# Key layouts made from one PSUM copy, and x tiles of the second layer pair turned by DMA, in a two-pair spectral and attention kernel

## The chip, the cores and the metric

The kernel runs on one core of a Trainium2 chip. The metric is device time in microseconds (us) of one execution; the kernel before takes 1351.86 us as the median of 4 runs (1351.64 to 1351.93). One of these executions, 1351.93 us, was also profiled, and all traces shown come from it.

## The reference: what is computed

The input x is 2048 rows by 512 columns in bf16. Two pairs of layers follow each other, and each layer adds its result to x. Weights are shared by the two pairs.

```python
x = A_x
x = x + _A_ref(_layernorm(x, axis=-1), A_w_r, A_w_i)
x = x + _B_ref(_layernorm(x, axis=-1), B_wq, B_wk, B_wv, B_wo)
x = x + _A_ref(_layernorm(x, axis=-1), A_w_r, A_w_i)
x = x + _B_ref(_layernorm(x, axis=-1), B_wq, B_wk, B_wv, B_wo)
```

`_A_ref` is a spectral filter: a real two-dimensional FFT over rows and columns, a product with the complex weight w_r + i w_i, and the inverse FFT. `_B_ref` is attention with 32 query heads of width 16 over one shared key and one shared value head, softmax over all 2048 keys, and an output projection:

```python
q = (lambda x, *d: x.transpose(*d))((x @ wq).reshape(B, S, H, Dh), 0, 2, 1, 3)
k = x @ wk
v = x @ wv
scores = jnp.einsum("bhqd,bkd->bhqk", q, k) * (Dh ** -0.5)
p = _softmax(scores, axis=-1)
o = jnp.einsum("bhqk,bkd->bhqd", p, v)
```

## The kernel before, in words

**Data.** x stays in SBUF as `x_sb`, [128 partitions, R = 4, T = 4, 512]: 16 tiles of 128 rows, addressed (t, r). There are eight PSUM banks: two double banks `sa`, and four single banks `b` (NB = 4). The bulk of the SBUF scratch is a pool `w4`; 13 small buffers `e2` hold exponentials and, for short times, other things; a pool `xnt` of six buffers holds normalised tiles.

**The spectral layer (A).** The front works on pairs of tiles. `tr_x` (L1064) turns two tiles with eight TensorE transposes into one `b` bank, `tr_evac` (L1070, which copies through the helper at L1236) takes them to an `e2` buffer, and `mm1` (L1076) multiplies each turned tile with the table PH, four matmuls into one `b` bank. `mm1_evac` (L1084) takes that out on ScalarE with the layer norm's scale, which comes from the statistics `bn` (L1015, VectorE) and `rstd` (L1030, ScalarE). Four tiles of one t are combined on VectorE (`radix_g`). The middle (`mid`, `filt`, `radix_d`) transforms along the rows, filters, and starts the inverse; the back (`inv`, `radix_v`, `y_mm`) finishes it and adds the result to x. For each t the back then normalises (`apply`, L1040, VectorE), turns again (`tr_n`, L1229), and makes keys, queries and values.

**The keys.** `k_mm` (L1249) makes, for the 512 rows of one t, a bank in which the 16 key rows are repeated eight times over the partitions. `k_evac` (L1253) takes that bank out twice, once into KA and once into KB, each time with a 0/1 column `part` that keeps the even or the odd groups of 16 partitions. One of the two is run on ScalarE and one on VectorE, whichever the planner finds free (`flex`, L797; ScalarE's form is L1256, VectorE's L1258). This happens for t = 0 to 3 in each pair of layers. Values follow (`v_mm`, `v_evac` with L1270 and L1272).

**The attention layer (B).** There are 32 blocks (four query stretches qb, four groups g, two parities), and each takes 16 key tiles times four heads, a unit being one 128x512 score tile. ScalarE takes two units at a time from an `sa` bank and exponentiates them (L1297). VectorE takes one unit from a `b` bank and makes a power-of-two approximation of the exponential from integer arithmetic (L1304); GpSimd adds two further phases of it (L1308). TensorE makes scores (L1292) and multiplies with the values (L1314) into one accumulator bank per block. When a block is done its bank is taken out by L1321. When four groups of a qb are done, `close_rows` (L879) projects (L1345), adds to x (L1227, `close_x`), and in the first pair starts the next layer's front on those rows, while attention goes on. So the front of the second pair runs inside the first attention for t = 0, 1, 2, and after it for t = 3.

**What sets the order.** Nothing is scheduled by hand: `Plan` simulates the engines with fixed durations, and emits each instruction when its simulated engine would start it. Every engine then executes its own list in order. Tasks are added with `add`: an engine or several (`ways`), a duration, dependencies, `take` (a PSUM bank it needs) and `give` (a bank it releases), `prio` and `order`. `both` (L188) releases a bank once two tasks have ended. `bg_next` (L240) picks the next background task; tasks of order above 20 are put back by TIER x (order - 20) / 10 nanoseconds, and the back's orders are 20 + 10 t and up. `pe_next` (L380) decides between scores, value matmuls and background matmuls: a background task that would overrun the due time of the next scores is cut into parts that fit, with a tolerance SLIP (100 ns) or, until VectorE has begun on softmax units, SLIP_RAMP (1200 ns). VectorE begins with them (`dve_on`) once the values of all four t are out; I call the time from the first back task to then the ramp. A task that has been late for PATIENT (1000 ns) may go in single parts. `fill` (L454) puts in dummy matmuls (L1002, L1006) to hold the TensorE clock up; one needs a free `b` bank or the accumulator.

**DMA.** SP's queue loads x, the weights, and the tables FT and w (`load_u`, L1103) and IT (`load_it`, L1161) of each pair, and in the last pair writes the output rows from `close_x` (L1351). A DRAM pool `way` of two buffers is declared and not used.

Of the kernel before, what the change touches and what calls it, by code (L numbers as in the profile page):

```python
# [8 lines left out]
ACT = mybir.ActivationFunctionType  # L9
ALU = mybir.AluOpType  # L10
P = 128
BF = mybir.dt.bfloat16
# [3 lines left out]
S, D, H, DH = 2048, 512, 32, 16  # L16
NF = D // 2 + 1
NT = 16
NC = 4
R = 4  # L20
T = 4
# [77 lines left out]
class Task:  # L99
# [5 lines left out]
    def __init__(self, eng, dur, deps, fn, take=None, give=(), then=None, prio=-1, order=0, lazy=0.0, gap=0.0, parts=1, port=False, lock=False, cols=None):  # L105
        self.ways = {eng: dur} if isinstance(eng, str) else dict(zip(eng, dur))
        self.eng, self.deps, self.fn = next(iter(self.ways)), deps, fn
        self.dur = self.ways[self.eng]
        self.take, self.give, self.then = take, give, then
        self.port, self.lock = port, lock  # L110
        self.cols = self.dur * 512.0 / 220.0 if cols is None else cols
        self.prio, self.order, self.lazy, self.gap, self.parts, self.step = prio, order, lazy, gap, parts, 0
        self.end = self.slot = None


class Plan:
# [21 lines left out]
    RAMP_FORCE = 3900.0  # L138
    HOLD = 200.0
    NB = 4  # L140
    TIER = 200.0
    LATE = 0.0
    GAP = 0.0
    SLIP = 100.0
    SLIP_RAMP = 1200.0
    PATIENT = 1000.0
    URGE = 150.0
    TURN = 7000.0
# [91 lines left out]
    def bg_next(self, eng):  # L240
        best = None
        for k in self.bg[eng]:
# [20 lines left out]
            elif eng == "PE" and self.t[eng] - max(ready, k.born) > self.STARVED:  # L263
                prio = -3
            c = (start + self.TIER * max(0, k.order - 20) // 10, prio, k.order, k.seq, start, k)
            if best is None or c[:4] < best[:4]:
# [113 lines left out]
    def pe_next(self):  # L380
# [21 lines left out]
        for b in self.bg_next("PE"):  # L402
            k, n = b[3], 99
            late = T - max(b[5], k.born)
            if kinds and c[0][0] <= b[0] + k.dur + self.PE_SW:
                room = max(limit, c[0][0]) + (self.SLIP if self.at.dve_on else self.SLIP_RAMP) - b[0] - self.PE_SW
                fit = int(room / (k.dur / k.parts)) if room > 0 else 0
# [270 lines left out]
class Layer:  # L678
# [15 lines left out]
    def __init__(self, plan, em, first, last):  # L694
        self.plan, self.em, self.first, self.last = plan, em, first, last
        self.next = None
        self.at = Attn(plan, em, self)
        self.rs = {}
        self.Pk, self.G, self.FT, self.W, self.Dz, self.IT, self.UT, self.V, self.sb, self.xn, self.xt = ({} for _ in range(11))
        self.mm1_done = {}  # L700
        self.g_done = {}
        self.stat = {}
        self.gate = []
        self.two, self.direct = ((x[0] if first else x[1]) for x in (self.TWO, self.DIRECT))
        self.sd_of = {}
# [95 lines left out]
    def add_back(self):  # L801
        p, em, at = self.plan, self.em, self.at
        left = [T]
        for t in range(T):
            o = 20 + 10 * t
            cs = []
            for b in range(2):
                es = []
                for j in range(2):
                    if t == 0 and not self.direct:  # L810
                        m = p.add("PE", 440.0, [self.mid[2 * j]], lambda k, t=t, b=b, j=j: em.inv(self, t, b, j, k.slot, (0,)),
                                  take="b", order=o)
                        n = p.add("PE", 440.0, [m, self.mid[2 * j + 1]],
                                  lambda k, t=t, b=b, j=j, m=m: em.inv(self, t, b, j, m.slot, (1,)), order=o)
                    elif t == 0:
                        m = p.add("PE", 880.0, [self.fil[2 * j]], lambda k, b=b, j=j: em.inv0(self, b, j, k.slot, 0),
                                  take="b", order=o)
                        n = p.add("PE", 880.0, [m, self.fil[2 * j + 1]],
                                  lambda k, b=b, j=j, m=m: em.inv0(self, b, j, m.slot, 1), order=o)
                    else:  # L820
                        n = m = p.add("PE", 880.0, self.mid, lambda k, s, t=t, b=b, j=j: em.inv(self, t, b, j, k.slot, (s,)),
                                      parts=2, take="b", order=o)
                    es.append(p.add(*self.flex(t, 482.0, 600.0), [n], lambda k, t=t, b=b, j=j, m=m: em.inv_evac(self, t, b, j, m.slot, k.eng),
                                    give=(m,), order=o))
# [3 lines left out]
            for j in range(0, R, w):  # L828
                key, ks = ("b", t, j), []
                for i, r in enumerate(range(j, j + w)):  # L830
                    put = t in self.FIRST_PUT
                    n = 5 if put else 4
                    y = p.add("PE", 217.0 * n, cs, lambda k, s, t=t, r=r, n=n: em.y_mm(self, t, r, k.slot, s, n), parts=n, take="b",
                              order=o + 1)
                    if put:
                        c = p.add("ACT", 482.0, [y], lambda k, t=t, r=r, y=y: em.put_x(t, r, y.slot), order=o + 1)
# [5 lines left out]
                    z = p.add("DVE", 597.0, [y], lambda k, t=t, r=r, y=y: em.add_x(t, r, y.slot), give=(y,), order=o + 1)  # L842
                    ks.append(p.add("DVE", 795.0, [z], lambda k, key=key, i=i, t=t, r=r, w=w: em.bn(self, key, i, (t, r), w),
                                    order=o + 2))
# [4 lines left out]
                for a in range(j, j + w, 2):  # L849
# [3 lines left out]
                                    lambda k, t=t, a=a, x=x: em.trn_evac(self, t, a, x.slot, k.eng), give=(x,), order=o + 4))  # L853

            def k_got(k, t, i):
                at.k_ready[(t, i)] = k.end + p.LAT[k.eng]
# [7 lines left out]

            m = p.add("PE", 870.0, te, lambda k, s, t=t: em.k_mm(self, t, k.slot, s), parts=4, take="b", order=o + 5)
            last = []
            for i in range(2):
                last.append(p.add(*self.flex(t, 586.0, 667.0), [m], lambda k, t=t, i=i, m=m: em.k_evac(t, i, m.slot, k.eng), order=o + 5))
            p.both(*last, m, lambda k, t=t, last=last: k_got(k, t, last.index(k)))
            if t == 0:  # L870
                at.add_qt((0, 0), te, o + 5)
            m = p.add("PE", 800.0, te, lambda k, s, t=t: em.v_mm(self, t, k.slot, s), parts=4, cols=256.0, take="b", order=o + 6)
# [6 lines left out]
    def close_rows(self, qb, deps):  # L879
        p, em, at = self.plan, self.em, self.at  # L880
        t = qb
        if not self.last and t == T - 1:
            p.ranked(1)
        rows = []
        for r in range(R):
            if t == T - 1:
                m = p.add("PE", 660.0, deps[:3] + [self.at.evac_last], lambda k, r=r: em.proj(at, t, r, k.slot, 0, 3), take="b",
                          prio=-2)
                if not self.last and self.PUTC:
                    n = p.add("PE", 434.0, [m, deps[3]], lambda k, r=r, m=m: (em.proj(at, t, r, m.slot, 3, 5), em.mm_x(t, r, m.slot)),  # L890
                              prio=-2)
                    n.put = m
                    rows.append(n)
                    continue
                n = p.add("PE", 220.0, [m, deps[3]], lambda k, r=r, m=m: em.proj(at, t, r, m.slot, 3, 4), prio=-2)
                rows.append(p.add("DVE", 597.0, [n], lambda k, r=r, m=m: em.close_x(self, t, r, m.slot), give=(m,), prio=-2))
                continue
            m = p.add("PE", 870.0, deps, lambda k, s, r=r: em.proj(at, t, r, k.slot, s, s + 1), parts=4, take="b", prio=-2, gap=p.GAP)
            z = p.add("DVE", 597.0, [m], lambda k, r=r, m=m: em.close_x(self, t, r, m.slot), give=(m,), prio=-2)
            rows.append(z)  # L900
        if self.last:
            return
        n = self.next
        w = 2 if t == T - 1 else R
        for j in range(0, R, w):
            n.add_stats(("f", t, j), [(t, r) for r in range(j, j + w)], rows[j:j + w])
        rows = [r.x if hasattr(r, "put") else r for r in rows]
        for j in range(0, R, 2):
            n.add_front([(t, j), (t, j + 1)], rows[j:j + 2], 1)
        if t == T - 1:  # L910
            n.gate = [at.taken]
            n.add_middle()
            n.add_back()
            p.ranks = None


class Emit:
# [130 lines left out]
    def load_x(self, L):  # L1048
        for t in range(T):
            self.nc.sync.dma_start(out=self.x[:, :, t], in_=self.xv[:, :, t])  # L1050

    def load_w(self, L):
        for u in range(2):
            self.load_u(L, u)
        for dst, src in self.w_dma:
            self.nc.sync.dma_start(out=dst, in_=src)
# [193 lines left out]
        self.nc.tensor.matmul(self.ps(slot), lhsT=self.wk8[:, c, :], rhs=self.xTc(L.at, t, c), start=(c == 0), stop=(c == NC - 1),  # L1250
                              skip_group_check=True)

    def k_evac(self, t, i, slot, eng):  # L1253
        out, part = (self.KA, self.KB)[i][:, 512 * t:512 * t + 512], self.part[:, i:i + 1]
        if eng == "ACT":
            self.nc.scalar.activation(out=out, in_=self.ps(slot), func=ACT.Identity, scale=part)  # L1256
        else:
            self.nc.vector.tensor_scalar(out=out, in0=self.ps(slot), scalar1=part, scalar2=None, op0=ALU.mult)  # L1258

    def v_mm(self, L, t, slot, r):  # L1260
        for c in range(NC):
# [174 lines left out]
```

## Time and profile before

| | |
|---|---|
| median of 4 runs | 1351.86 us |
| profiled execution | 1351.93 us |
| its span, first to last instruction | 1350.1 us |
| granted TensorE clock | 1.000 |
| PE busy | 1311.2 us (97%) |
| DVE busy | 1299.9 us (96%) |
| ACT busy | 1224.9 us (91%) |
| POOL busy | 850.6 us (63%) |
| DMA moved | 22.02 MB, mean 16 GB/s |

PE is TensorE, DVE VectorE, ACT ScalarE, POOL GpSimd, SP SyncE; PEld is TensorE's weight load, which overlaps PE. Matmuls are pipelined and PE's busy time includes dummies, so 97% does not say that TensorE is at its peak. A line such as L1236 can be a helper that several tasks use; the tile names left of the arrow tell which. The stages can be told from the busy digits: the first pair's spectral work until about 58 us, its ramp to 110, its attention to 686; the second pair's spectral work to 730, ramp to 782, attention to 1340, and a short end. Lines of a timeline give the start in us, the length in us, engine, line, operation, output and input, count, and in brackets the idle time just before and what ended it. A length is that of a group of merged instructions where the count is over one.

### The profile page before, as it was taken

The numbers are of one execution on the slowest core, as the hardware profiler recorded it, in microseconds if no ns is written. First come the engines' busy times: TensorE is split into PE (matmuls) and PEld (weight loads), VectorE is DVE, ScalarE is ACT, GpSimd is POOL, SyncE is SP. The second block draws the span as 40 slices with busy tenths as digits, with TensorE's granted clock in tenths as the row PEclk, the third lists the DMA queues.
The fourth block names the chain that finished last, engine by engine and source line by source line (L and its number), as shares of the span: only waits on it lengthen the run. The fifth ranks groups of instructions, "written<-read, shape, count | busy, mean of one in ns | idle before, by whom it ended". The sixth has DMA issues, their size and how long they took to land.

```text
span 1350.1 us, 31719 instructions
## 1 busy us (share of the span) xinstructions
PE 1311.2 (97%) x13051; PEld 429.5 (32%) x13118; DVE 1299.9 (96%) x2328; ACT 1224.9 (91%) x1390; POOL 850.6 (63%) x834
## 2 busy tenths in 40 slices
PE   9999999999999999999999999999999999999998
PEld 4642222222223222222246422222222222322222
DVE  6998999999999999999979989999999999999998
ACT  6479999989999899999964799998999999998996
POOL 0005777667776677766820057776777767876775
PEclk9999999999999999999999999999999999999999
DMA  9100000000000000000051000000000000000000
GB/s 290 40 1 1 2 1 2 2 1 1 2 1 2 1 2 2 1 1 2 2 164 40 1 1 2 2 2 17 1 2 1 6 13 2 1 1 18 1 2 17
DMA packets 21073, 22.02 MB, mean 16 GB/s; under 512 B 2240, under 2 KB 19648, under 8 KB 20928
## 3 DMA queue, kind: packets, MB, share of 16 engines
q1 hardware_dynamic: 20640, 19.44, 4.6%
q8 instruction: 102, 1.67, 0.5%
q10 hardware_dynamic: 288, 0.56, 0.1%
q14 instruction: 43, 0.35, 0.1%
HBM read 17.89 MB, written 2.10 MB: 15 GB/s over the span
## 4 chain that ended last, share of the span: by engine, by line
DVE 33%; ACT 31%; PE 30%; issue 3%; DMA 1%; SPq 1%; POOL 0%; POOLq 0%; DVEq 0%
ACT e L1297 31%; DVE w L1304 22%; PE b L1314 12%; PE sa L1292 6%; PE b L1292 6%; DVE st L1020 2%; DVE w L1149 1%; DVE x_sb L1227 1%; PE b L1345 1%; PE b L1276 1%; DVE raw L1321 1%; PE b L1078 1%; PE b L1176 1%; DVE on L1332 1%; DVE xd L58 1%
## 5 line engine op out<-in xcount | busy, mean ns | idle before, releaser
L1297 ACT ACTIVATE e<-sa 128x1024 bf16<-128x1024 f32 x1228 | 1138.5, 1080 | 34.3 <-PE sa L1292 27.1
L1308 POOL INT64_ADD w<-w x818 | 847.6, 1048 | 480.4 <-DVE w L1304 436.0
L1304 DVE TENSOR_SCALAR w<-b 128x512 uint16<-128x512 f32 x1640 | 1000.9, 679 | 8.1 <-PE b L1292 2.9
L1314 PE MATMUL b<-w,vs 128*32 128x512 bf16 x4920 | 543.3, 385 | 4.2 <-DVE w L1310 1.1
L1314 PE MATMUL b<-e,vs 128*32 128x512 bf16 x2456 | 406.1, 386 | 0.3
L1292 PE MATMUL b<-w,KB 32*128 32x512 bf16 x852 | 262.2, 381 | 3.3 <-DVE w L1304 1.2
L1292 PE MATMUL sa<-w,KA 32*128 32x512 bf16 x1260 | 258.0, 382 | 5.8 <-ACT e L1297 3.4
L1292 PE MATMUL sa<-w,KB 32*128 32x512 bf16 x1196 | 248.0, 381 | 5.4 <-ACT e L1297 2.3
L1314 PEld LDWEIGHTS <-vs 128*32 128x32 bf16 x7376 | 144.3, 94 | 338.4 <-issue 322.5
L1292 PE MATMUL b<-w,KA 32*128 32x512 bf16 x788 | 232.1, 381 | 0.5
L1292 PEld LDWEIGHTS <-KA 32*128 32x128 bf16 x2048 | 81.0, 91 | 226.0 <-issue 217.6
L1292 PEld LDWEIGHTS <-KB 32*128 32x128 bf16 x2048 | 82.4, 91 | 221.7 <-issue 217.0
L1321 DVE STREAM_TRANSPOSE raw<-b 128x512 f32<-128x512 f32 x64 | 45.2, 706 | 2.4 <-PE b L1314 2.4
L1020 DVE BATCH_NORM_STATS2 st<-x_sb 128x6 f32<-128x512 bf16 x52 | 35.4, 681 | 4.8 <-DMA x_sb<-in_A_x_dram 4.3
L1227 DVE TENSOR_TENSOR x_sb<-b,x_sb 128x512 bf16<-128x512 f32 x52 | 34.5, 678 | 3.5 <-PE b L1345 2.7
L1276 PE MATMUL b<-gx,wq 128*128 128x512 bf16 x103 | 34.6, 385 | 0.6
L1345 PE MATMUL b<-WO,w 128*128 128x512 bf16 x114 | 33.2, 382 | 0.8 <-DVE w L1341 0.2
L1176 PE MATMUL b<-it,xd 128*128 128x256 bf16 x256 | 30.8, 273 | 3.2 <-DVE xd L58 3.2
L1216 PE MATMUL b<-tab_PS,w 128*128 128x512 bf16 x120 | 31.5, 379 | 1.2 <-DVE KB L1258 0.8
L1078 PE MATMUL b<-tab_PH,e 128*128 128x512 bf16 x119 | 30.5, 380 | 1.7 <-ACT w L1091 0.3
L1236 ACT CAST e<-b 128x512 bf16<-128x512 f32 x30 | 17.1, 586 | 15.0 <-PE b L1176 9.8
L1091 ACT ACTIVATE w<-b,sb 128x512 bf16<-128x512 f32 x32 | 21.3, 689 | 9.5 <-PE b L1078 8.0
(84 smaller groups left out, 590.1 us busy)
## 6 DMA issues: line engine op xcount, KB each, us to landing
it<-const_IT SPq DMA_DIRECT2D x8, 640.0 KB, 6.3
w<-const_FT SPq DMA_DIRECT2D x8, 512.0 KB, 7.4
x_sb<-in_A_x_dram SPq DMA_DIRECT2D x4, 512.0 KB, 7.5
w<-in_A_w_r_dram SPq DMA_DIRECT2D x8, 256.0 KB, 6.9
w<-in_A_w_i_dram SPq DMA_DIRECT2D x8, 256.0 KB, 7.3
out_dram<-x_sb SPq DMA_DIRECT2D x16, 128.0 KB, 1.8
tab_PH<-const_PH ACTq DMA_DIRECT2D x1, 512.0 KB, 5.7
tab_PS<-const_PS SPq DMA_DIRECT2D x1, 512.0 KB, 7.9
```

The lines of the kernel that those rows point to most:

```text
L1020: self.nc.vector.bn_stats(st, self.ps(slot) if slot else self.x[:, x[1], x[0], :])
L1078: self.nc.tensor.matmul(self.ps(slot), lhsT=xt[:, cc, P * i:P * i + P], rhs=self.PH[:, cc, :], start=(cc == 0), stop=(cc == NC - 1), skip_ ...
L1176: self.nc.tensor.matmul(ps[:, k, :], lhsT=z, rhs=L.IT[t][:, u, w:w + 256], start=(a == 0 and i == 0), stop=(a == 1 and i == 1), skip_group ...
L1227: self.nc.vector.tensor_tensor(out=x, in0=self.ps(slot), in1=x, op=ALU.add)
L1276: self.nc.tensor.matmul(self.ps(slot), lhsT=self.wq[:, c, g * 128:(g + 1) * 128], rhs=self.xTc(at, qb, c), start=(c == 0), stop=(c == NC - ...
L1292: self.nc.tensor.matmul(o, lhsT=KX[rs, kc * P:(kc + 1) * P], rhs=at.QT[qb][rs, g, :], start=True, stop=True, skip_group_check=True)
L1297: self.wrote("ACT", e, self.nc.scalar.activation(out=e, in_=self.ps(slot), func=ACT.Exp, scale=SCALE))
L1304: self.nc.vector.tensor_scalar(out=t[0][:, j], in0=self.ps(slot), scalar1=P1_SCALE, scalar2=P1_BIAS, op0=ALU.mult, op1=ALU.add)
L1308: self.nc.gpsimd.int64_add(t[p][:, 0:n].bitcast(U64), t[0][:, 0:n].bitcast(U64), DELTA[p] * FOUR)
L1314: self.nc.tensor.matmul(self.ps(slot)[32 * h:32 * h + 32, :], lhsT=V[:, kc, :], rhs=rhs, start=first, stop=last, skip_group_check=True)
L1321: self.nc.vector.transpose(out=at.raw[(qb, g)][:, par].rearrange("p a b -> p (a b)"), in_=self.ps(slot))
L1345: self.nc.tensor.matmul(self.ps(slot), lhsT=at.OT[t][:, g, r * P:(r + 1) * P], rhs=self.WO[:, g, :], start=(g == 0), stop=(g == g1 - 1), s ...
```

## The change

Four things change in the text.

1. `k_evac` copies the key bank once, as it is, into a buffer of the `xnt` pool, on ScalarE or VectorE; the bank is released then. Two VectorE instructions (`k_part`) make KA and KB from that SBUF copy. The scores of a t may start when the planner's `k_part` has ended.
2. In the first pair, each pair of rows that `close_rows` closes at t = 0, 1, 2 is written by a DMA from SP to the DRAM pool `way` and read back by a transposing DMA from SP into an `e2` buffer. `add_front` then leaves out `tr_x` and `tr_evac` for that pair; `mm1` is planned from 7 us (TURN, which was there) after the second close. t = 3 is turned by TensorE as before, and so are all tiles of the first pair.
3. TIER goes from 200 to 150.
4. SLIP_RAMP goes from 1200 to 600.

```diff
-    TIER = 200.0
+    TIER = 150.0
...
-    SLIP_RAMP = 1200.0
+    SLIP_RAMP = 600.0
...
             m = p.add("PE", 870.0, te, lambda k, s, t=t: em.k_mm(self, t, k.slot, s), parts=4, take="b", order=o + 5)
             last = []
+            c = p.add(*self.flex(t, 482.0, 600.0), [m], lambda k, t=t, m=m: em.k_evac(self, t, m.slot, k.eng), give=(m,), order=o + 5)
             for i in range(2):
-                last.append(p.add(*self.flex(t, 586.0, 667.0), [m], lambda k, t=t, i=i, m=m: em.k_evac(t, i, m.slot, k.eng), order=o + 5))
-            p.both(*last, m, lambda k, t=t, last=last: k_got(k, t, last.index(k)))
+                p.add("DVE", 323.0, [c], lambda k, t=t, i=i: em.k_part(self, t, i), then=lambda k, t=t, i=i: k_got(k, t, i), order=o + 5)
...
+        turned = [Mark("DMA", None) for _ in range(2)]
+
+        def closed(k):
+            j = rows.index(k) // 2
+            if not self.last and all(z.end is not None for z in rows[2 * j:2 * j + 2]):
+                em.turn_x(self.next, [(t, 2 * j), (t, 2 * j + 1)])
+                turned[j].end = k.end + p.TURN
...
-            z = p.add("DVE", 597.0, [m], lambda k, r=r, m=m: em.close_x(self, t, r, m.slot), give=(m,), prio=-2)
+            z = p.add("DVE", 597.0, [m], lambda k, r=r, m=m: em.close_x(self, t, r, m.slot), give=(m,), then=closed, prio=-2)
...
-            n.add_front([(t, j), (t, j + 1)], rows[j:j + 2], 1)
+            n.add_front([(t, j), (t, j + 1)], rows[j:j + 2], 1, turned[j // 2] if t < T - 1 else None)
...
+    def turned(self, L, tiles, rows):
+        xt = self.t2([NC, 2 * P])
+        self.writer.pop(self.home[id(xt)][0], None)
+        self.nc.sync.dma_start_transpose(out=xt, in_=rows)
+        L.xt[tuple(tiles)] = [xt, 2 * NC]
+
+    def turn_x(self, L, tiles):
+
+        (t, r), _ = tiles
+        way = self.way.tile([2 * P, D], BF, name="way")
+        self.nc.sync.dma_start(out=way.rearrange("(r p) d -> p r d", r=2), in_=self.x[:, r:r + 2, t, :])
+        self.turned(L, tiles, way)
...
-    def k_evac(self, t, i, slot, eng):
-        out, part = (self.KA, self.KB)[i][:, 512 * t:512 * t + 512], self.part[:, i:i + 1]
-        if eng == "ACT":
-            self.nc.scalar.activation(out=out, in_=self.ps(slot), func=ACT.Identity, scale=part)
-        else:
-            self.nc.vector.tensor_scalar(out=out, in0=self.ps(slot), scalar1=part, scalar2=None, op0=ALU.mult)
+    def k_evac(self, L, t, slot, eng):
+        L.K8[t] = self.pool.tile([P, 512], BF, name="xnt", tag="xnt", bufs=6)
+        self.copy(eng, L.K8[t], self.ps(slot))
+
+    def k_part(self, L, t, i):
+
+        self.nc.vector.tensor_scalar(out=(self.KA, self.KB)[i][:, 512 * t:512 * t + 512], in0=L.K8[t], scalar1=self.part[:, i:i + 1],
+                                     scalar2=None, op0=ALU.mult)
```

More of the change, by code (lines that the diff above doesn't have):

```diff
@@ L698, in __init__ @@
         self.rs = {}
-        self.Pk, self.G, self.FT, self.W, self.Dz, self.IT, self.UT, self.V, self.sb, self.xn, self.xt = ({} for _ in range(11))
+        self.Pk, self.G, self.FT, self.W, self.Dz, self.IT, self.UT, self.V, self.sb, self.xn, self.xt, self.K8 = ({} for _ in range(12))
         self.mm1_done = {}
```

## The prediction

> **What bounds the kernel now.** I began with the table by stretch of time, which gives each engine's busy time in windows laid along the stages. Its columns are the window, its length, and then PE, PEld, DVE, ACT and POOL with their instruction counts, the granted clock, the DMA share and GB/s.
>
> ```profile
> 58.00:110.00 52.00, 49.31 (x410) 25.80 (x416) 46.67 (x139) 38.42 (x57) 0.00 (x0) 1.00 0.09 26
> 110.00:262.00 152.00, 149.34 (x1567) 41.86 (x1572) 150.85 (x255) 150.88 (x164) 115.72 (x112) 1.00 0.01 2
> 262.00:304.00 42.00, 40.85 (x392) 12.12 (x396) 41.66 (x75) 34.99 (x41) 25.30 (x27) 1.00 0.01 2
> ...
> 922.00:942.00 20.00, 19.04 (x160) 5.61 (x161) 19.17 (x32) 16.16 (x19) 12.38 (x13) 1.00 0.09 28
> ```
>
> The reader is to see three kinds of stage. In plain attention (110 to 262 us) VectorE and ScalarE are both 99% busy: they share the softmax units, so the two together are the bound and time freed on one is shared out. At a row close of the first attention (262 to 304) VectorE stays full while ScalarE loses 7.0 us. In the ramp (58 to 110) VectorE is nearly full and ScalarE loses 13.6 us, GpSimd does nothing. The granted clock is 1.00 throughout.
>
> Next the page's groups, for what a unit costs, and the rows that the change touches, from the groups kept apart by shape (busy, mean ns, then idle before and its releaser).
>
> ```profile
> L1297 ACT ACTIVATE e<-sa 128x1024 bf16<-128x1024 f32 x1228 | 1138.5, 1080 | 34.3 <-PE sa L1292 27.1
> L1304 DVE TENSOR_SCALAR w<-b 128x512 uint16<-128x512 f32 x1640 | 1000.9, 679 | 8.1 <-PE b L1292 2.9
> ```
> ```profile
> L1236 DVE COPY e<-b 128x1024 bf16<-128x1024 bf16 x8 | 5.4, 680 | 0.5 <-PE b L1068 0.3
> L1256 ACT ACTIVATE KA<-b,part 128x512 bf16<-128x512 f32 x6 | 4.2, 692 | 4.7 <-PE b L1250 4.7
> L1258 DVE TENSOR_SCALAR KB<-b,part 128x512 bf16<-128x512 f32 x6 | 4.5, 748 | 1.0 <-ACT KA L1256 1.0
> ```
>
> Means overlap at their ends, so I take start-to-start intervals from the timeline: 12 exponentials in 11.31 us and 47 in 43.40, that is 0.923 us for two units, 0.462 us a unit on ScalarE; 16 units in 9.81 us on VectorE, 0.609 each. One microsecond freed on VectorE is therefore worth 0.462 / (0.462 + 0.609) = 0.43 us of time, one freed on ScalarE 0.57 us.
>
> Last the timeline at two places: the first row close, and the end of the ramp.
>
> ```profile
> 279.88 0.71 DVE L1321 STREAM_TRANSPOSE raw<-b 128x512 f32<-128x512 f32 x1
> 280.02 0.61 PE L1068 MATMUL b<-tab_ident,x_sb 128*128 128x128 bf16 x8 [0.22 <-DVE w L1304]
> ...
> 281.09 0.67 DVE L1236 COPY e<-b 128x1024 bf16<-128x1024 bf16 x1
> 281.22 0.61 PE L1068 MATMUL b<-tab_ident,x_sb 128*128 128x128 bf16 x8
> ...
> 282.05 0.81 PE L1078 MATMUL b<-tab_PH,e 128*128 128x512 bf16 x3 [0.22 <-DVE e L1236]
> ```
> ```profile
> 107.07 1.02 PE L1250 MATMUL b<-gx,wk 128*128 128x512 bf16 x3 [0.45 <-DVE gx L1236]
> ...
> 108.13 0.75 DVE L1258 TENSOR_SCALAR KA<-b,part 128x512 bf16<-128x512 f32 x1 [1.12 <-PE b L1250]
> ...
> 108.92 0.69 ACT L1256 ACTIVATE KB<-b,part 128x512 bf16<-128x512 f32 x1 [1.73 <-DVE KA L1258]
> ...
> 109.66 0.38 PE L1002 MATMUL b<-zero 128*128 128x512 bf16 x1 [0.73 <-ACT KB L1256]
> ```
>
> In the first, the rows were closed by 266.2 us (the last L1227 of t = 0), yet the turning starts at 280.0, right after L1321 has freed an accumulator's bank: PSUM banks, not the rows, start it. From there to 289.05 no value matmul (L1314) runs, because front work holds the banks, and ScalarE runs dry. In the second, the two masked key copies are taken one after the other by different engines out of one bank, and TensorE's next matmul waits 0.73 us for the second.
>
> **The x tiles of layer two.** For t = 0, 1, 2 the change takes away six turnings: six times eight transposes (0.61 us of PE each time) and six copies L1236, one VectorE instruction each, 0.60 us from start to start (281.09 to 281.69). VectorE: 6 x 0.60 = 3.6 us, worth 3.6 x 0.43 = **1.55 us**; all of it lies in full stages. TensorE: 6 x 0.61 = 3.7 us plus two bank turns per t. What that gives ScalarE I size from the idle at the closes. ScalarE idles 7.0 us in 262 to 304, 6.5 in 422 to 465, 5.4 in 568 to 622, 18.9 together; the second attention, whose closes have no front, idles 3.84, 1.06 and 2.64 in its three windows (922, 1080, 1222), 7.5 together. The excess, 11.4 us, is the front's. Of the front's TensorE work per t (1.22 us of turning, 4 x 0.87 of L1078) the turning is 26%: 3.0 us of ScalarE, x 0.57 = **1.7 us**. Ends: 0, if the mm1 matmuls take the same banks just as long, and 11.4 x 0.57 = 6.5 if the whole knot loosens. I take 1.7 as the proportional share. What is late next at a close is mm1 and its ScalarE evacuation (L1091 waits 8.0 us for L1078 in all).
>
> What is added per pair: SP issues a 256 KB write to DRAM and then a turning read of 256 KB back, the second waiting for the first to land. No turning DMA is in this trace. Its nearest rows: a 128 KB output write lands in 1.8 us, the 640 KB table in 6.3; so a leg lies between 1.8 and 6.3, a pair between 3.6 and 12.6, and by size between the rows a leg is 1.8 + 4.5 x 128/512 = 2.9, a pair 5.8 plus two issues of 0.33 (the output writes' issue) = 6.5 us. The plan allows 7. Queued behind on SP there is only the second pair, and long after it the tables of layer two (SP's L1105 waits 615 us for a buffer today). Only at t = 1 do the pairs crowd: the second and fourth L1227 start at 422.4 and about 424.5; the second pair's read then lands some 10 us after 422.4, 0.9 us past its plan. Cost taken: 0. Cover: today's first mm1 starts 21, 8 and 10 us after the first pair's second close (282.1, 431.0, 583.1 against 261.3, 423.0, 572.8), since banks and statistics come later than the rows. Without that cover an in-order TensorE would stand, with scores and values behind it, for whatever is over 7 us plus the 1.85 us that two queued exponentials last. DMA share there is 0.01, so the engines are free.
>
> A rule speaks against this part: the Trainium skill, VectorE: DVE Perf Modes, section The three transpose paths, gives 390 ns for a 128x128 block on TensorE and 1309 ns through the DMA crossbar. TensorE's figure is far above this trace, where eight take 0.61 us in a row; eight blocks at 1309 ns would be, as an estimate from that page, 10.5 us for the read alone, and the sum would lose its gain wherever mm1 is due at once. No run here shows the crossbar yet.
>
> **The keys**, four times per layer. Removed: one L1256 and one L1258 (ScalarE about 0.6, VectorE 0.66 from 85.38 on). Added: one plain copy (L1236 128x512: 586 ns on ScalarE, 677 on VectorE) and two SBUF-to-SBUF multiplies on VectorE of L1044's form, four of which take 1.38 us, 0.32 apart. VectorE: 0.64 for 0.66, nothing, if ScalarE copies; 0.6 more if VectorE does, as it would where it takes the first evacuation today (2 of 8, both at t = 3, where it idles 1.12 and 1.02 us). The second engine's turn at the bank goes: the bank is free about 0.7 us earlier, KA ready 0.2 to 0.4 later (another semaphore and 0.32), KB 0.1 to 0.2 earlier. At t = 3 the chain is 108.13, copy 0.60, multiply 0.32, about 0.25 to the scores: 109.3 where 109.97 stands now. V's evacuations (L1270, L1272; 0.68 us) slide behind the multiplies, so I take half, 0.3 us per layer, **0.6 us**; ends -0.3 and +0.65 per layer. The multiplies wait on the copy in VectorE's queue; at t = 0 to 2 there are other spectral pieces to put between, and without them each wait is 0.2 us.
>
> **Planner constants.** TIER 150 and SLIP_RAMP 600 work only on the order; the first on all back work of the ramp, the second lets scores push in front of background matmuls there. Instructions stay the same in number. VectorE's 5.3 us and ScalarE's 13.6 us of idle per ramp bound it: a gain of at most 13.6 x 0.57 = 7.8 per layer, and a loss by the last tile's chain, priced in (b). I take 0: VectorE's fixed work fills the ramp up to 94 us.
>
> **Sum**: 1.55 + 1.7 + 0.6 = 3.85 us. The profiled execution took 1351.93 us, a span of 1350.1 and 1.8 around it; 1351.93 - 3.85 = 1348.1, and as the median is 1351.86, **1348.0**.
>
> **Rivals.** (a) *Banks stay the knot*: transposes go, yet ScalarE starves as before since the four mm1 and projections hold the banks. Then 1.55 + 0.3 = 1.85: **1350.0**, no visible change (a measurement of this kernel tells about 0.2%, 2.7 us, from none). For it: turning waited 14 us for a bank. Against: each turning holds one from 280.0 past 281.7.
> (b) *The ramp's last tile comes later*, the slower side. With 600 ns of slip a background matmul of 0.87 us no longer fits past a due score. From 94 to 110 us VectorE is not covered (gaps 0.40, 0.51, 0.76, 0.64, 1.12, 1.02), and some eight matmul tasks of t = 3 lie on its chain; each behind one score round with its switches (0.22 + 2 x 0.1 planned) is 3.4 us per ramp, 6.7 in two, against 3.85: **1354.7**. It decides from 1.9 us a ramp. Against: the planner lets single parts through once a task is 1 us late.
> (c) *The turning lands late*: at 12.6 + 0.7 us, 13.3 - 8.85 = 4.4 us stand at each pair whose mm1 is due; if due for three of six, 13 - 3.85: **1361**. Against: the cover above. It decides at 8.85 + 3.85 / 6 = 9.5 us if all six are due.
> (d) *Done in name only* can't be for the transposes; for the keys it would be VectorE doing the copies too, 8 x 0.58 us x 0.43 = 2.0 off the gain: **1350.0**, counted with (a).
>
> **Chances.** Forecast 0.50 (its own range 1344 to 1349), (a) and (d) 0.27, (b) 0.15, (c) 0.08. So faster by over 0.2% 0.50, within 0.27, slower 0.23. The range: below, the whole knot, 1.55 + 6.5 + 0.6 = 8.6, gives 1343.3; above, past (b) to 1356; most of (c) is left out.
>
> **What would show it.** Right: L1068's count falls from 128 to 80; ScalarE's idle in the three closes falls by about 3 us; mm1 never waits for a DMA; the ramp's first L1304 some 0.3 us earlier. Wrong: idle of TensorE released by a DMA before mm1 (c); the first VectorE softmax unit after the ramp later than 110.4 us (b); unchanged idle at the closes (a); L1236 of the keys on VectorE (d).

## The result, and the profile after

The changed kernel takes 1349.42 us as the median of 40 runs (1348.89 to 1351.14), the kernel before 1351.81 us over 60 runs: 2.4 us less, a ratio of 0.9984 (95% interval 0.9980 to 0.9989). Forecast were 1348.0 us, 3.85 us less. The time lies in the range, but within the 0.2% that the prediction called no visible change. The profiled execution took 1349.44 us, its span is 1347.5.

First the table by stretch of time of the changed kernel (columns as before: window, length, PE, PEld, DVE, ACT, POOL, clock, DMA share, GB/s), then four windows of the kernel before that were not shown yet.

```profile
262.00:304.00 42.00, 41.23 (x408) 11.93 (x415) 41.84 (x73) 40.74 (x48) 28.59 (x28) 1.00 0.11 27
304.00:422.00 118.00, 114.21 (x1185) 33.59 (x1182) 116.97 (x201) 111.44 (x122) 87.34 (x86) 1.00 0.01 3
422.00:465.00 43.00, 42.09 (x413) 11.58 (x413) 39.89 (x74) 40.46 (x47) 26.04 (x27) 1.00 0.09 22
465.00:568.00 103.00, 100.47 (x1017) 29.05 (x1020) 102.42 (x175) 98.29 (x108) 78.00 (x76) 1.00 0.01 4
568.00:622.00 54.00, 53.38 (x545) 15.00 (x546) 50.80 (x90) 52.36 (x60) 35.25 (x36) 1.00 0.07 16
```
```profile
304.00:422.00 118.00, 115.59 (x1207) 32.44 (x1209) 117.45 (x199) 116.47 (x127) 90.97 (x88) 1.00 0.01 2
422.00:465.00 43.00, 42.08 (x409) 12.48 (x410) 41.24 (x75) 36.47 (x43) 25.58 (x27) 1.00 0.01 1
465.00:568.00 103.00, 101.33 (x1072) 28.86 (x1072) 102.50 (x173) 102.59 (x112) 79.94 (x78) 1.00 0.01 2
568.00:622.00 54.00, 53.09 (x527) 16.06 (x530) 53.35 (x94) 48.64 (x56) 35.97 (x36) 1.00 0.01 1
```

Read ACT against the window's length. At the three closes (262, 422, 568) ScalarE's idle fell from 7.0, 6.5 and 5.4 us to 1.3, 2.5 and 1.6: a gain of 13.5 us, if one looks no further. In the plain windows next to them (304, 465, and 622 to 686) it rose from 1.5, 0.4 and 0.1 to 6.6, 4.7 and 1.8, which is 11.1 us. Net 2.4 us went, and VectorE idled 3.9 us more in the windows 422 and 568 (39.89 and 50.80 busy, before 41.24 and 53.35). A window that looks cured can have handed its idle to the next.

The groups, ScalarE's softmax units first and then the rows that the change touches:

```profile
L1320 ACT ACTIVATE e<-sa 128x1024 bf16<-128x1024 f32 x1231 | 1141.5, 1093 | 45.2 <-PE sa L1315 40.8
```
```profile
L1089 PE MATMUL b<-tab_ident,x_sb 128*128 128x128 bf16 x80 | 5.6, 219 | 0.7 <-ACT x_sb L1244 0.7
L1257 ACT CAST xnt<-b 128x512 bf16<-128x512 f32 x6 | 3.5, 585 | 4.8 <-PE b L1271 4.8
L1280 DVE TENSOR_SCALAR KB<-xnt,part 128x512 bf16<-128x512 bf16 x8 | 2.8, 348 | 0.0
L1257 DVE COPY e<-b 128x1024 bf16<-128x1024 bf16 x2 | 1.3, 674 | 0.3 <-PE b L1089 0.3
```

Transposes went from 128 to 80, VectorE's copies of turned tiles from 8 to 2, and ScalarE makes six of the eight key copies. ScalarE's idle before exponentials rose from 34.3 to 45.2 us, released by TensorE's scores. Some of that has only moved: the idle before `mm1_evac` fell from 9.5 to 4.0 us. The DMA issues (KB, us from issue to landing):

```profile
way<-x_sb SPq DMA_DIRECT2D x6, 256.0 KB, 2.2
e<-way SPq DMA_TRANSPOSE x6, 3.3
```

Write and turned read land 5.5 us after their issues in sum, and no L1099 (mm1) waits for a DMA. Then the end of the first ramp, by the timeline:

```profile
105.55 0.69 DVE L1257 COPY gx<-b 128x1024 bf16<-128x1024 bf16 x1 [0.64 <-PE b L1254]
...
107.50 0.69 DVE L1257 CAST xnt<-b 128x512 bf16<-128x512 f32 x1 [1.26 <-PE b L1271]
...
108.23 0.35 DVE L1280 TENSOR_SCALAR KA<-xnt,part 128x512 bf16<-128x512 bf16 x1
...
108.64 0.39 PE L1315 MATMUL sa<-w,KA 32*128 32x512 bf16 x4 [0.46 <-DVE KA L1280]
...
109.28 0.68 DVE L1327 TENSOR_SCALAR w<-b 128x512 uint16<-128x512 f32 x1
```

VectorE's first softmax unit starts at 109.28 us, where it started at 110.43. With such starts I cut every profile into stages: first ramp (to VectorE's first softmax unit), first attention (to its last block's evacuation), the second pair's spectral work and ramp (to its first softmax unit), second attention, end. In us:

| | ramp 1 | attention 1 | between | attention 2 | end | span |
|---|---|---|---|---|---|---|
| before | 110.43 | 578.11 | 93.70 | 559.37 | 8.49 | 1350.1 |
| after | 109.28 | 576.60 | 92.49 | 560.89 | 8.24 | 1347.5 |
| turning alone | 110.32 | 573.79 | 93.71 | 559.14 | 8.24 | 1345.2 |
| keys alone | 110.46 | 580.73 | 93.85 | 565.08 | 8.48 | 1358.6 |
| constants alone | 110.84 | 581.58 | 94.04 | 562.51 | 8.53 | 1357.5 |
| turning, order kept | 110.38 | 575.43 | 93.68 | 558.90 | 8.21 | 1346.6 |
| keys, order kept | 109.56 | 577.89 | 92.66 | 559.01 | 8.48 | 1347.6 |

The changed kernel gains 1.15 and 1.21 us at the two ramps and 1.51 in the first attention, and loses 1.52 in the second, where VectorE, ScalarE and GpSimd have the same work as before and TensorE 11 dummy matmuls fewer. That loss was in no term of the sum. (The row of the constants alone comes from an execution 1.2 us above that kernel's median, with 3.4 us at half clock in its first attention.) My theory after this comparison: the edits earn about what they should, and the planner's new order, which any edit brings about, gives part of it back. By order I mean the whole layout that the planner makes: the sequence on each engine, which engine takes a softmax unit, and how many dummies are put in. The rival: one of the edits costs something by itself, by its instructions, waits or DMAs.

### The profile page after: what moved, and what is told of

It is laid out like the page before. It is cut to its first block, busy times and chain, and to the rows that moved or that the text cites. A ratio compares the mean times of both kernels' runs of the same rounds, so it can differ in the third digit from the quotient of the medians.

```text
span 1347.5 us, 31563 instructions
## 1 busy us (share of the span) xinstructions
PE 1308.7 (97%) x12963; PEld 434.0 (32%) x13031; DVE 1296.3 (96%) x2333; ACT 1222.6 (91%) x1387; POOL 848.5 (63%) x832
## 4 chain that ended last, share of the span: by engine, by line
ACT 44%; PE 31%; DVE 21%; issue 2%; DMA 1%; SPq 1%; POOL 0%; DVEq 0%; ACTq 0%; POOLq 0%
ACT e L1320 44%; DVE w L1327 13%; PE b L1337 10%; PE sa L1315 7%; PE b L1315 5%; DVE w L1170 1%; PE b L1197 1%; DVE st L1028 1%; PE b L1368 1%; PE b L1237 1%; PE b L1099 1%; PE b L1299 1%; DVE x_sb L1248 1%; DVE xd L58 1%; DVE raw L1344 1%
## 5 line engine op out<-in xcount | busy, mean ns | idle before, releaser
L1320 ACT ACTIVATE e<-sa 128x1024 bf16<-128x1024 f32 x1231 | 1141.5, 1093 | 45.2 <-PE sa L1315 40.8
L1327 DVE TENSOR_SCALAR w<-b 128x512 uint16<-128x512 f32 x1635 | 1000.3, 680 | 10.3 <-PE b L1315 5.9
L1315 PE MATMUL sa<-w,KA 32*128 32x512 bf16 x1252 | 252.5, 381 | 10.9 <-ACT e L1320 6.4
L1315 PE MATMUL sa<-w,KB 32*128 32x512 bf16 x1209 | 251.5, 381 | 5.0 <-ACT e L1320 2.3
L1315 PE MATMUL b<-w,KB 32*128 32x512 bf16 x839 | 252.7, 381 | 2.7 <-DVE w L1327 1.3
L1315 PE MATMUL b<-w,KA 32*128 32x512 bf16 x796 | 235.6, 381 | 0.6
L1315 PEld LDWEIGHTS <-KA 32*128 32x128 bf16 x2048 | 85.1, 91 | 223.5 <-issue 211.9
L1099 PE MATMUL b<-tab_PH,e 128*128 128x512 bf16 x117 | 29.9, 380 | 1.2 <-ACT w L1112 0.3
L1197 PEld LDWEIGHTS <-xd 128*128 128x128 bf16 x256 | 24.5, 98 | 8.5 <-DVE xd L58 3.9
L1010 PE MATMUL b<-zero 128*128 128x512 bf16 x69 | 23.2, 425 | 2.6 <-DVE eps L963 1.2
```

The costliest lines, as they stand in the source:

```text
L1197: self.nc.tensor.matmul(ps[:, k, :], lhsT=z, rhs=L.IT[t][:, u, w:w + 256], start=(a == 0 and i == 0), stop=(a == 1 and i == 1), skip_group ...
L1315: self.nc.tensor.matmul(o, lhsT=KX[rs, kc * P:(kc + 1) * P], rhs=at.QT[qb][rs, g, :], start=True, stop=True, skip_group_check=True)
L1320: self.wrote("ACT", e, self.nc.scalar.activation(out=e, in_=self.ps(slot), func=ACT.Exp, scale=SCALE))
L1327: self.nc.vector.tensor_scalar(out=t[0][:, j], in0=self.ps(slot), scalar1=P1_SCALE, scalar2=P1_BIAS, op0=ALU.mult, op1=ALU.add)
```

## The experiments

### Each part alone, and in pairs

The parts of the diff as it stands: turning (item 2) in the first, keys (item 1) in the second, the constants (items 3 and 4) in the third, then the three pairs.

```diff
-            n.add_front([(t, j), (t, j + 1)], rows[j:j + 2], 1)
+            n.add_front([(t, j), (t, j + 1)], rows[j:j + 2], 1, turned[j // 2] if t < T - 1 else None)
```

> The DMA turning alone, on the kernel before. If the time comes from the freed work (theory): 1.55 us of VectorE's share and 1.7 of ScalarE's, 1348.6 us. If only VectorE's share counts and the banks stay the knot: 1350.2. If the change's gain sits in the keys or the constants: 1351.5 to 1352. If the order of the work by itself scatters the time by some microseconds (rival): anything between 1348 and 1354, with no relation to the sum. L1068's counterpart should count 80, and no mm1 should wait for a DMA, since write and turned read took 2.2 and 3.3 us in the changed kernel.

Measured: 1347.05 us, ratio 0.9966 [0.9954, 0.9979]. That is 4.55 less than before, and 2.4 less than the whole change: it beats both kernels.

```diff
+            c = p.add(*self.flex(t, 482.0, 600.0), [m], lambda k, t=t, m=m: em.k_evac(self, t, m.slot, k.eng), give=(m,), order=o + 5)
...
+                p.add("DVE", 323.0, [c], lambda k, t=t, i=i: em.k_part(self, t, i), then=lambda k, t=t, i=i: k_got(k, t, i), order=o + 5)
```

> The key copy alone, on the kernel before. Theory: the ramp's first VectorE softmax unit some 0.3 to 1.1 us earlier than 110.43 in each pair (in the changed kernel it starts at 109.28), VectorE and ScalarE both gain it, so 0.6 to 2.2 us: 1349.6 to 1351.2. Rival, order scatter: the ramp ends earlier and the time doesn't follow.

Measured: 1360.42 us, 1.0069 [1.0056, 1.0082], 8.8 us slower than before, where 0.6 to 2.2 us were to be gained. The ramp did not get shorter either: VectorE's first softmax unit is at 110.46 us. The table puts the loss into the attentions (2.62 and 5.71 us), where there is no key work at all: every key is made in a ramp.

```diff
-    TIER = 200.0
+    TIER = 150.0
...
-    SLIP_RAMP = 1200.0
+    SLIP_RAMP = 600.0
```

> TIER 150 and SLIP_RAMP 600 alone, on the kernel before. No instruction is added or taken away, so every difference is order. Theory: within 0.5 us of 1351.8, and the ramp's first softmax unit on VectorE within 0.3 us of 110.43. Rival (the ramp's last tile comes later): up to 3.4 us later per ramp. Rival, order scatter: 1 to 3 us either way.

Measured: 1358.11 us, 1.0047 [1.0034, 1.0061], 6.5 us slower. The ramps are 0.41 and 0.34 us longer; the attentions, where neither constant acts, 3.47 and 3.14, some 1.2 of the first by the half clock. More dummies are not the reason: there are 58 in these attentions, against 60 before.

```diff
-                last.append(p.add(*self.flex(t, 586.0, 667.0), [m], lambda k, t=t, i=i, m=m: em.k_evac(t, i, m.slot, k.eng), order=o + 5))
+            c = p.add(*self.flex(t, 482.0, 600.0), [m], lambda k, t=t, m=m: em.k_evac(self, t, m.slot, k.eng), give=(m,), order=o + 5)
...
-            n.add_front([(t, j), (t, j + 1)], rows[j:j + 2], 1)
+            n.add_front([(t, j), (t, j + 1)], rows[j:j + 2], 1, turned[j // 2] if t < T - 1 else None)
```

> Turning and keys without the two constants. If the parts add: the time of the kernel before plus the two differences of the runs with one part each, and the constants account for the rest to 1349.4. If order scatter rules: off that sum by more than 1.5 us.

Measured: 1358.11 us, 1.0050 [1.0038, 1.0063]. The two single differences would add up to 1355.9; the pair is 2.2 us above.

```diff
-    TIER = 200.0
+    TIER = 150.0
...
-    SLIP_RAMP = 1200.0
+    SLIP_RAMP = 600.0
...
-                last.append(p.add(*self.flex(t, 586.0, 667.0), [m], lambda k, t=t, i=i, m=m: em.k_evac(t, i, m.slot, k.eng), order=o + 5))
+            c = p.add(*self.flex(t, 482.0, 600.0), [m], lambda k, t=t, m=m: em.k_evac(self, t, m.slot, k.eng), give=(m,), order=o + 5)
```

> The changed kernel with layer two's tiles turned by TensorE again. Against it the changed kernel shows the turning's worth in its own surroundings. Theory (the freed work is worth 3.2 us, more or less the same everywhere; so far 4.6 on the kernel before, 2.3 beside the keys): 1352.6 us, 1351.5 to 1354. Rival, the order decides and the turning's worth isn't a constant: outside 1350 to 1355.

Measured: 1355.03 us, 1.0017 [1.0008, 1.0026]. Its executions fall into two groups, five at 1352.5 to 1352.7 us, where the theory had it, and six at 1355.0 to 1356.9; the profiled one is of the second and shows why, in these windows:

```profile
451.09:457.92 6.83, 6.59 (x31) 2.06 (x31) 3.26 (x5) 2.62 (x3) 3.74 (x4) 0.50 0.00 0
458.00:460.00 2.00, 2.00 (x11) 0.88 (x9) 1.39 (x2) 0.17 (x1) 0.29 (x1) 1.00 0.00 0
```

The third column from the right, the granted clock, is at a half for 6.83 us, at a close where ScalarE and VectorE both starve.

```diff
-    TIER = 200.0
+    TIER = 150.0
...
-    SLIP_RAMP = 1200.0
+    SLIP_RAMP = 600.0
...
-            n.add_front([(t, j), (t, j + 1)], rows[j:j + 2], 1)
+            n.add_front([(t, j), (t, j + 1)], rows[j:j + 2], 1, turned[j // 2] if t < T - 1 else None)
```

> Turning with the two constants, without the keys. Theory of a constant worth: 3.2 us below the constants alone (1358.1), 1354.9, 1353.5 to 1356. If keys and constants only work together because each alone spoils the order by chance, this run can lie anywhere from 1349 to 1358.

Measured: 1353.68 us, 1.0017 [1.0008, 1.0026].

With before (as it ran beside the single parts) and after this makes all eight combinations (medians in us):

| | neither | keys | constants | both |
|---|---|---|---|---|
| without turning | 1351.6 | 1360.4 | 1358.1 | 1355.0 |
| with turning | 1347.1 | 1358.1 | 1353.7 | 1349.4 |
| difference | -4.6 | -2.3 | -4.4 | -5.6 |

Turning gains in every column, by 4.2 on the mean. Keys and constants don't add: +8.8 and +6.5 alone, +3.2 together (against before as it ran beside that pair, 1351.8), or +0.7 if the six executions with a half clock are left out; turning's last column is then -3.1 and the mean 3.6. A cost that sits in an instruction would be about the same in each column. What varies is then likely to be in how the instructions are laid out.

### Is it the order? Two edits of one nanosecond in the plan

A planned duration is changed by one nanosecond, and nothing is changed in what a task does. The plan that comes of it is more than ties falling otherwise: ScalarE has 1230 and 1229 exponentials in the two kernels (1228 before), VectorE 1637 and 1638 softmax units (1640), and the dummies at L1002 and L1006 are 61 and 52 in the first, 68 and 64 in the second (60 and 52).

```diff
-    ACT_EXP = 908.0
+    ACT_EXP = 909.0
```

> A null edit of the kernel before: the planner's duration of an exponential is 909 ns in place of 908. Nothing is computed or placed differently, only ties in the plan fall otherwise. If order scatter is what moved the keys and the constants by +8.8 and +6.5 us: differs from 1351.6 by several us, either way. If those two have causes of their own and order scatter is small: within 1 us of 1351.6.

Measured: 1352.21 us, 1.0005 [0.9997, 1.0014], 0.4 us above before.

```diff
-    DVE_P1 = 600.0
+    DVE_P1 = 601.0
```

> A second null edit of the kernel before: the planner's duration of VectorE's softmax unit is 601 ns in place of 600. As for the first: several us either way if order scatter rules, within 1 us of 1351.6 if not. If both null edits land above the kernel before, its constants are at a favourable point of the scatter, and an edit on it starts with a handicap.

Measured: 1355.74 us, 1.0026 [1.0015, 1.0036]: 3.9 us slower; by the profile 2.8 of it lies in the first attention. The three executions at full clock are at 1354.4, which is 2.6 us; the other four are 1.3 us or more longer, and in the profiled one of them the clock is at half from 944.73 to 948.14 us. So a new layout, with its own chance of a half clock, can cost as much as the whole forecast. Both such edits land above the kernel before, whose order seems a lucky one; two edits are few to say it.

```diff
-    DVE_P1 = 600.0
+    DVE_P1 = 601.0
...
-            n.add_front([(t, j), (t, j + 1)], rows[j:j + 2], 1)
+            n.add_front([(t, j), (t, j + 1)], rows[j:j + 2], 1, turned[j // 2] if t < T - 1 else None)
```

> The turning on top of the second null edit (601 ns), a fifth surrounding for its worth. Theory of 3.7 us on the mean of four (2.3 to 5.6 so far): 1351.2 from 1354.4, the undipped runs of that null edit, 1349 to 1353. Rival, a gain that belongs to the order of one kernel alone: at 1354 or above.

Measured: 1350.63 us, 0.9990 [0.9981, 0.9999]. Against the same order edit without turning that is 5.1 us less (5.3 between the executions at full clock): turning's worth holds on another base too.

### Each edit with the order kept

Here the planner of the kernel before is left alone, with its tasks and durations, so the order is that of before. The tasks of turning stay in the plan for t = 0, 1, 2 but issue nothing; the DMA pair is issued at the second close. In the trace ScalarE's 1390 and GpSimd's 834 instructions follow each other as before, and VectorE's do too but for the six copies.

```diff
     def tr_x(...):
+        if tuple(tiles) in L.xt:
+            return
...
     def tr_evac(...):
+        if tuple(tiles) in L.xt:
+            return
```

> The turning with the order of the kernel before: the planner still counts transposes and copies, so every engine keeps its list, and only the 48 transposes and six copies are left out of it; the tiles come by DMA. This is the freed work without a new order. Theory of the prediction: VectorE's 1.55 us surely, of ScalarE's 1.7 the part that is shorter bank turns; 1348.6 to 1350.2. Rival, the gain of 4.6 us is the new order's: 1351 to 1352. Rival, the mm1 wait for the DMA: above 1352, with TensorE idle released by a DMA.

Measured: 1348.37 us, 0.9975 [0.9965, 0.9985], 3.4 us less, and no mm1 waits for a DMA. ScalarE's busy time at the three closes rose by 1.06, 0.73 and 0.41 us. The first of these windows in this kernel:

```profile
262.00:304.00 42.00, 40.86 (x381) 11.26 (x382) 41.63 (x75) 36.05 (x42) 26.44 (x28) 1.00 0.11 27
```

The knot stays: 6 of the 7 us of idle at the first close are still there. What ScalarE waits for is mm1, as it was before, and only the wait for a turned copy is gone; the timeline of its instructions says so (start, length, and in brackets the idle before), first two lines of the kernel before, then this kernel:

```profile
283.02 0.69 ACT L1091 ACTIVATE w<-b,sb 128x512 bf16<-128x512 f32 x1 [0.99 <-DVE e L1236]
285.16 0.69 ACT L1091 ACTIVATE w<-b,sb 128x512 bf16<-128x512 f32 x1 [1.45 <-PE b L1078]
```
```profile
284.05 0.69 ACT L1116 ACTIVATE w<-b,sb 128x512 bf16<-128x512 f32 x1 [1.26 <-PE b L1103]
285.34 0.69 ACT L1116 ACTIVATE w<-b,sb 128x512 bf16<-128x512 f32 x1 [0.60 <-PE b L1103]
287.19 0.69 ACT L1116 ACTIVATE w<-b,sb 128x512 bf16<-128x512 f32 x1 [1.16 <-PE b L1103]
288.70 2.85 ACT L1322 ACTIVATE e<-sa 128x1024 bf16<-128x1024 f32 x3 [0.83 <-PE sa L1317]
```

L1116 is `mm1_evac` and L1103 `mm1` in this kernel. The keys next: the two tasks of before are kept; the first makes the SBUF copy on its engine and then its masked half on VectorE, the second only its half on VectorE.

```diff
     def k_evac(self, L, t, i, slot, eng):
+        if t not in L.K8:
+            L.K8[t] = self.pool.tile([P, 512], BF, name="xnt", tag="xnt", bufs=6)
+            self.copy(eng, L.K8[t], self.ps(slot))
+        self.nc.vector.tensor_scalar(out=(self.KA, self.KB)[i][:, 512 * t:512 * t + 512], in0=L.K8[t], scalar1=self.part[:, i:i + 1],
+                                     scalar2=None, op0=ALU.mult)
```

> The keys' new path with the order of the kernel before: where the first of the two evacuations stood, the plain copy and KA's multiply; where the second stood, KB's multiply on VectorE. Theory of the prediction: 0.6 us gained or nothing, 1351 to 1352; the ramp's first VectorE softmax unit earlier than 110.43. Rival, the instructions themselves cost the 8.8 us of the keys alone: 1356 to 1360. If this run is at 1351 to 1352, the 8.8 us are the new order's.

Measured: 1349.19 us, 0.9981 [0.9972, 0.9990], 2.6 us less, where the same path in a new order is 8.8 more. The expectation was 0.6 or nothing. So the path itself costs nothing in the attentions (0.22 and 0.36 us less there) and gains 0.87 and 1.04 at the ramps. The end of its first ramp:

```profile
105.97 0.69 DVE L1236 COPY gx<-b 128x1024 bf16<-128x1024 bf16 x1 [0.64 <-PE b L1233]
...
107.78 0.69 DVE L1236 CAST xnt<-b 128x512 bf16<-128x512 f32 x1 [1.11 <-PE b L1250]
...
108.50 0.35 DVE L1257 TENSOR_SCALAR KA<-xnt,part 128x512 bf16<-128x512 bf16 x1
...
109.34 1.02 ACT L1297 ACTIVATE e<-sa 128x1024 bf16<-128x1024 f32 x1 [2.51 <-PE sa L1292]
109.56 0.68 DVE L1304 TENSOR_SCALAR w<-b 128x512 uint16<-128x512 f32 x1
```

From the last copy of turned rows (`gx`) to the first softmax unit it takes 3.59 us, against 4.10 before (106.33 to 110.43): 0.51 us by KA and KB no longer taken in turn out of one bank. The other 0.36 is there already when `gx` starts (105.97 against 106.33), from the earlier t. VectorE and ScalarE both wait on this chain (the brackets), so a microsecond here is one of the total, not 0.43.

VectorE shows what a new order does: in the first attention it idles 5.4 us before, and 5.8 and 5.1 in the two kernels of this section. In every kernel planned anew it idles 9.4 us or more there (10.3 in the changed kernel, 13.4 with the keys alone).

### Is the DMA's cover real?

Turning alone, with mm1 planned 2 us after the second close instead of 7.

```diff
-    TURN = 7000.0
+    TURN = 2000.0
...
-            n.add_front([(t, j), (t, j + 1)], rows[j:j + 2], 1)
+            n.add_front([(t, j), (t, j + 1)], rows[j:j + 2], 1, turned[j // 2] if t < T - 1 else None)
```

> Turning alone, but the planner allows 2 us from the second close to mm1 in place of 7; write and read take 2.2 and 3.3 us and their issues 0.4, so mm1 planned at once would stand 3.9 us, 2 us past what ScalarE has queued. If banks and statistics cover it as in the prediction: no TensorE idle released by a DMA and a time like another order of the turning alone, 1346 to 1350. If it is due at once (the prediction's rival of the late landing): idle of 2 to 4 us at some of the six, and 1349 to 1357.

Measured: 1365.47 us, 1.0098 [1.0082, 1.0113], 18.4 us above turning alone and above both ranges expected. The waits (engine and line, what it waited for, us in total, times, longest), the timeline and a window of this kernel:

```profile
PE b L1099 <- DMA e<-way: 7.8, 3, 4.4
```
```profile
425.54 1.23 SPq L1063 DMA_TRANSPOSE e<-way  x1
...
428.72 1.03 PE L1099 MATMUL b<-tab_PH,e 128*128 128x512 bf16 x2 [4.36 <-DMA e<-way]
```
```profile
427.64:437.88 10.24, 9.16 (x50) 1.67 (x50) 4.09 (x7) 4.48 (x7) 2.05 (x2) 0.50 0.26 61
```

TensorE stands in order before mm1, as rival (c) had it, until the read issued at 425.54 has landed 3.2 us later. Then comes what (c) did not have: the clock is granted at half from 427.64, 3.3 us into this stand, to 437.88, though PE is busy again from 428.72 on, and all engines run behind it. At the third close it happens again, for 6.83 us. The waits make 7.8 us; 15.2 us of TensorE's busy time at half rate are, as an estimate from these rows, 7.6 more; the loss in the first attention is 20.6. In the profiled execution of the changed kernel neither happens.

## Why the prediction came out as it did

The time came within 1.4 us of the forecast in part by luck: the keys' term was 2.0 us too small, and that covers over half of what order, taken as 0, gave back.

**The step that failed is "Planner constants ... I take 0"**, and with it the silent assumption that the first two edits leave the order alone. With the order kept, turning gives 3.4 us and keys 2.6, together 6.0 if they add, which wasn't tried in one kernel; the change gives 2.4. So about 3.6 us go back by order (some 2 to 5.5, by the three intervals). The bound stood for order in the ramps only (7.8 gain, 3.4 loss each); order acts through all 1137 us of attention, and keys alone or constants alone lose 8.3 and 6.6 us there. A nanosecond on one planned duration is worth 2.6 us at full clock and 3.9 by the median. Nor do the instructions "stay the same in number": the constants alone have 73 and 32 dummies in the whole kernel, where before has 60 and 52.

**Turning** was sized well: 3.25 predicted, 3.4 at fixed order. By its parts: VectorE's six copies went; ScalarE's idle at the closes fell by 2.2 us instead of 3.0, so 1.55 + 2.2 x 0.57 = 2.8, and the first attention of that kernel is 2.68 shorter. Of the rest, 0.28 lies in the end, as in every kernel with turning (8.2 us against 8.5), and 0.47 in the second attention; I have no cause for either. The share of 26% was near enough. (Of the two intervals behind the weights, 12 in 11.31 us would be 0.94 us, not 0.923; the weights hardly move.) In the kernel as changed I take the whole first attention, before and after:

```profile
110.43:688.54 578.11, 566.60 (x5845) 162.35 (x5868) 572.73 (x977) 554.55 (x608) 423.86 (x415) 1.00 0.02 6
```
```profile
109.28:685.88 576.60, 563.34 (x5771) 162.72 (x5797) 566.29 (x968) 556.69 (x611) 421.28 (x412) 1.00 0.04 11
```

VectorE was freed of 3.6 us but idles 4.9 more (10.3 against 5.4), ScalarE idles 3.7 less (19.9 against 23.6): 1.55 - 4.9 x 0.43 + 3.7 x 0.57 = 1.5, as measured. In the second attention the same count gives 0.6 of the 1.52 us lost (VectorE idles 0.3 less, ScalarE 1.3 more); for the rest I have no cause.

The Trainium skill's figure (VectorE: DVE Perf Modes, The three transpose paths), as an estimate 10.5 us for the eight blocks of a read, is not what these runs show: the read lands in 3.3 us. The measurement decides.

**The keys** were the mis-sized term: 0.6 predicted, 2.6 at fixed order. I had the last tile's chain right in kind, at 0.65 us, and halved it for the values' evacuations sliding behind; 0.51 of it came, and the earlier tiles of the ramp gave 0.36 more. VectorE copies 2 of 8, as expected.

**DMA** was estimated at 6.5 us a pair, with issues, and is 5.6 to its landing in the first pair (issues at 269.88 and 272.19, 3.3 from the second). The cover was there: mm1 began 9.6 us after that second close.

**Rivals.** (a) has the number, 1350.0 against 1349.4, but not the mechanism: ScalarE did gain at the closes at fixed order, and the keys were worth four times their term. It is half right in that the mm1 matmuls keep most of the knot. (b) fell: the ramp ends 1.15 us earlier. The constants alone do make it later, by 0.41 us and not by 3.4; with keys they end it earlier (109.08 us in the pair of the two). (c) is real, as the 2 us plan shows, and was covered. (d) did not happen. Of the signs, the transposes' count and mm1's waits came as named. The sign "idle in the three closes falls by about 3 us" would have misled: it fell by 13.5 and was handed on.

Open remain: by what rule the new orders starve VectorE and ScalarE more, what the constants are worth apart from the order that they bring, and whether both edits with the order kept would reach 1345.8 (1351.8 - 6.0). Turning alone in its own order, 1347.05, is the fastest kernel run here.

## What to carry to other kernels

Where a planner lays out the instructions, an edit changes two things, its own work and the order of everything; price the second by a null edit of the plan, and size the first with the order kept, before either is believed. Sum idle over a close and its neighbours, since a knot that dissolves in one window can be handed to the next. A microsecond is worth its whole self where both engines wait on one chain, and only its share where they split the work.

## What the runs showed of the chip

In the 2 us plan TensorE's granted clock fell to half 3.3 us into a stand of 4.36 us, and was full again only 9.2 us after TensorE had gone on. It also fell where no such stand is shown: for 6.83 us in the pair of keys and constants, and for 3.41 us in four kernels, one of them the constants alone:

```profile
379.52:382.94 3.42, 3.28 (x22) 0.64 (x25) 2.25 (x5) 1.82 (x3) 2.05 (x2) 0.50 0.00 0
```

The Trainium skill (TensorE: Matmul & The Clock Gate, Part 1: The HAM clock gate (the "warmup" mystery)) has two rates, half and full, and full again after about 3.4 us of sustained activity. The two rates are what the rows show, and the four short stretches have that length; the three others, one in the pair and two in the 2 us plan, last two or three times as long, though PE is shown busy for most of them.

A DMA that turns 256 KB from DRAM into SBUF landed 3.3 us after its issue, against 2.2 for the plain write of the same size, and held SP for 1.23 us against 0.38.
